# Feature map of a linear-attention branch: min-max on GpSimd, then one fused max-add on VectorE that reads PSUM

## The chip, the cores and the metric

The kernel runs on one core of a Trainium2 chip. A core has a matrix engine (TensorE, PE in the profile), three elementwise engines (VectorE or DVE, ScalarE or ACT, GpSimd or POOL), a queue engine for transfers (SyncE or SP), an on-chip memory of 128 partitions (SBUF) and a matmul result memory of eight banks of 128 x 512 float32 (PSUM). Each engine works through its own instruction list in order; engines wait for each other on semaphores. The metric is the device time of one execution in microseconds (us).

## The reference

Two attention blocks read the same input x (2048 tokens of 512 values, 32 heads of 16) and are mixed by a gate per token. Block A is softmax attention; block B is linear attention with a feature map phi.

```python
def _B_ref(x, wqkv, wo):
    ...
    phi = lambda t: jnp.where(t > 0, t + 1, jnp.exp(t)) + 1e-6
    pq, pk = phi(q), phi(k)
    kv = jnp.einsum("bhsd,bhse->bhde", pk, v)
    z = jnp.einsum("bhsd->bhd", pk)
    num = jnp.einsum("bhqd,bhde->bhqe", pq, kv)
    den = jnp.einsum("bhqd,bhd->bhq", pq, z)[..., None] + 1e-6
    o = num / den
    ...
x = A_x
g = _sigmoid((x * gate_w).sum(-1, keepdims=True))
a = _A_ref(x, A_wqkv, A_wo)
b = _B_ref(x, B_wqkv, B_wo)
return g * a + (1 - g) * b
```

`_A_ref` is plain softmax attention: scores, softmax, weighted sum of v, output projection.

## The kernel before

Most of the work is block A. Its scores are cut into 2048 units of 128 keys x 512 queries of one head. A unit's scores come from one matmul (source Qz, KT; "S" below), which uses 32 rows of the matrix engine, so up to four units run beside each other in one wave. The exponential of a unit is taken on one of two ways:

- on ScalarE: two units at a time out of a pair of PSUM banks, line 750, into a tile P. Banks 0, 1 and 2, 3 are two sets that alternate.
- by bit arithmetic: VectorE adds a constant to one unit and stores it as int16 (line 671, from bank 4 or 5, into a tile Z); read as bfloat16 this is a rough power of two. For each pair of units two shifted copies are then made (line 723 on GpSimd, or line 728 on VectorE), and the weighted sum of the three is the exponential. One pair of units therefore needs two instructions of line 671 and two shifts, wherever these run.

P and Z tiles are then multiplied by v (source P,Vc or Z,Vc; up to four units to a wave, into bank 7). A pair of units on ScalarE gives two such matmuls, a pair on the other way six.

All else is written as *tasks*: Python generators that yield one step at a time, a matmul group on PE or one instruction on another engine, with the tiles it reads and writes. Tasks are the projections of q, k and v, the gate, the 16 maps phi(k) (`t_phik`), the products MT, Z and KV, the 16 maps phi(q) (`t_phiq`), denominators and outputs of block B, and the 16 output blocks (`t_final`, lines 1120 to 1156). A task takes its PSUM bank by ("BANK",) and gives it back by ("FREE", b). While scores are being issued, bank 6 is the one bank that tasks share, so a bank that is held longer holds up the next task; at the end of the score work the other banks are added.

No order is written by hand. A planner in the kernel (the loop from line 1336) keeps a clock for each engine, takes the candidates (S waves, both ways of the exponential, shifts, products with v, task steps), gives each a start by its operands' due times and by the cost that stands in the source as the first argument of `ac`, `dv` and `po`, and appends the one with the earliest start to its engine's list. Which units take which way is decided there, by which engine is free. Gaps on PE are filled with matmuls on a tile `warm` whose result is not used. GpSimd instructions and VectorE's shifts (line 728) are planned so that they don't overlap, and a GpSimd instruction waits for the VectorE instruction ahead of the last shift (`gate`, lines 299 and 1388). A change of one cost or step thus gives a new order on every engine from there on.

The feature map is the generator `phi` (lines 1019 to 1028), which `t_phik` and `t_phiq` run for a 128 x 512 block in bank b: ScalarE writes exp(t) to `eb` (line 1023), VectorE writes max(t, 0) + 1e-6 to `mb` (line 1024) and the bank is free, GpSimd clamps `eb` to at most 1 (line 1026), and GpSimd adds the two into `phiK` (line 1027). There are two buffers of `eb` and of `mb`, so two maps may be under way; `mb` also holds the gate's transposes (line 969).

Of the kernel before, what the change touches and what calls it, by code (L numbers as in the profile page):

```python
# [8 lines left out]
ALU = mybir.AluOpType  # L9
# [117 lines left out]
def bass_gated_mix__mha_block__linear_attn_block__prompt_kernel(  # L127
# [46 lines left out]
    with ExitStack() as es:  # L174
        _cnt = [0]

        def SB(shape, dt, name):
            _cnt[0] += 1
            return es.enter_context(nc.sbuf_tensor(f"{name}_{_cnt[0]}", list(shape), dt))
# [37 lines left out]
        eb = SB([128, 2, 512], FP32, "eb")  # L217
        mb = SB([128, 2, 512], FP32, "mb")
# [13 lines left out]
        def bank(b, n=1):  # L232
            return ps[:, 512 * b:512 * (b + n)]
# [8 lines left out]
        r_bank = [R(f"bank{b}") for b in range(8)]  # L242
# [18 lines left out]
        r_eb = [R(f"eb{i}") for i in range(2)]  # L261
        r_mb = [R(f"mb{i}") for i in range(2)]
# [589 lines left out]
        def dv(dur, fn, reads, writes):  # L852
            return ("OP", DV, dur, fn, reads, writes, None)

        def ac(dur, fn, reads, writes):
            return ("OP", AC, dur, fn, reads, writes, None)

        def po(dur, fn, reads, writes):
            return ("OP", PO, dur, fn, reads, writes, None)
# [159 lines left out]
        def phi(b, dst_ap, dst_res):  # L1019
            yield ("WAIT", lambda: phi_free[0] or phi_free[1])  # L1020
            i = 0 if phi_free[0] else 1
            phi_free[i] = False
            yield ac(480, lambda: nc.scalar.activation(eb[:, i, :], bank(b), ACT.Exp), [r_bank[b]], [r_eb[i]])  # L1023
            yield dv(607, lambda: nc.vector.tensor_scalar(mb[:, i, :], bank(b), 0.0, 1e-6, op0=ALU.max, op1=ALU.add), [r_bank[b], r_eb[i]], [r_mb[i]])  # L1024
            yield ("FREE", b)
            yield po(640, lambda: nc.gpsimd.tensor_scalar(eb[:, i, :], eb[:, i, :], 1.0, 0.0, op0=ALU.min, op1=ALU.max), [r_eb[i]], [r_eb[i]])  # L1026
            yield po(1300, lambda: nc.gpsimd.tensor_tensor(dst_ap, eb[:, i, :], mb[:, i, :], ALU.add), [r_eb[i], r_mb[i]], dst_res)  # L1027
            phi_free[i] = True

        def t_phik(tb):  # L1030
            b = yield ("BANK",)
            for h in range(2):
                yield pe_step(2, 512, [mmt(bank(b), xT[:, cc, 128 * tb:128 * (tb + 1)], wB[:, cc, D:2 * D], start=(cc == 0), stop=(cc == NCC - 1))
                                       for cc in (2 * h, 2 * h + 1)], [r_xT[tb // 4][h], r_wB], [r_bank[b]])
            yield from phi(b, phiK[:, tb, :], [r_phiK[tb]])
            yield ("FLAG", lambda: flags.add(("phik", tb)))
# [38 lines left out]
        def t_phiq(qc, i):  # L1075
            yield ("WAIT", lambda: "z" in flags and "kv" in flags)
            b = yield ("BANK",)
            for h in range(2):
                yield pe_step(2, 512, [mmt(bank(b), wB[:, cc, 128 * i:128 * (i + 1)], xT[:, cc, 512 * qc:512 * (qc + 1)], start=(cc == 0), stop=(cc == NCC - 1))
                                       for cc in (2 * h, 2 * h + 1)], [r_xT[qc][h], r_wB], [r_bank[b]])  # L1080
            yield from phi(b, phiQT[:, 4 * qc + i, :], [r_phiK[4 * qc + i]])
            yield ("FLAG", lambda: flags.add(("phiq", qc, i)))
# [253 lines left out]
        while True:  # L1336
# [53 lines left out]
            if isinstance(c.fns, tuple) and c.fns[0] == "DMA":  # L1390
                _, o, i, sem, tot, lat, rd, wr, tr, chk = c.fns[1]
# [72 lines left out]
```

The softmax here doesn't subtract the row's maximum and nothing guards it: scores larger than these inputs give would overflow.

## Time and profile before

| | |
|---|---|
| median of 5 runs | 690.05 us (689.82 to 690.58) |
| the profiled execution | 690.04 us, of which the span from its first to its last instruction is 688.1 us |
| granted clock of TensorE | 1.000 |
| units of scores on ScalarE (line 750) | 707 instructions of two units each |
| units on the other way (line 671) | 634, with 408 shifts on GpSimd and 226 on VectorE |
| the 32 feature maps | 32 instructions each at lines 1023, 1024, 1026 and 1027 |

The page of the profile gives busy time by engine, the busy share in 40 slices of the span, the chain of work that ended last, and groups of equal instructions (line, engine, operation, written tile <- read tiles, shape, count | busy us, mean ns of one | idle time of that engine just ahead of them, and what ended it). Instructions of one engine overlap at their ends, so a mean duration can be longer than the distance from one to the next. Busy time counts an overlap once.

### The profile page before, as it was taken

To read this page: it belongs to the slowest core of one execution; us is meant where nothing else is said; L and a number is where in the kernel's file an instruction comes from. 1 tells how busy PE (TensorE), PEld (TensorE's weight loads), DVE (VectorE), ACT (ScalarE), POOL (GpSimd) and SP (SyncE) were. 2 spreads that over 40 slices of the span, in tenths; PEclk is the share of its full clock that TensorE was granted. 3 is DMA by queue.
4 is the path that set the end of the run, shared out by engine and by line. 5 is a ranking of instruction groups with operands and counts; after the bars stand their busy time and mean duration, and the time that the engine had idled before them with its cause. 6 is when DMAs were issued, how large, how long until landed. Compare 5 with 4: busy or idle time off the path is not lost.

```text
span 688.1 us, 24162 instructions
## 1 busy us (share of the span) xinstructions
PE 671.5 (98%) x9890; PEld 204.8 (30%) x9923; DVE 607.4 (88%) x1084; ACT 669.2 (97%) x746; POOL 536.8 (78%) x600
## 2 busy tenths in 40 slices
PE   8999999999999999999999999999999999999998
PEld 3323232222323232222333323232333322222222
DVE  6899989889988898988889888989889899988995
ACT  5899999999999999999999999999999999999995
POOL 3748888887898879886887888878989985588860
PEclk9999999999999999999999999999999999999999
DMA  6920000000000000000000000000011210000001
GB/s 132 304 62 10 7 5 7 2 10 1 5 8 2 9 4 1 10 2 10 2 11 3 4 9 2 10 2 3 17 25 34 49 25 25 17 10 16 18 17 40
DMA packets 27869, 15.97 MB, mean 23 GB/s; under 512 B 19696, under 2 KB 26736, under 8 KB 27760
## 3 DMA queue, kind: packets, MB, share of 16 engines
q1 hardware_dynamic: 26416, 13.91, 7.5%
q8 instruction: 79, 1.29, 0.8%
q10 hardware_dynamic: 1344, 0.52, 0.3%
q14 instruction: 30, 0.25, 0.1%
HBM read 6.69 MB, written 2.10 MB: 13 GB/s over the span
## 4 chain that ended last, share of the span: by engine, by line
PE 64%; ACT 23%; issue 9%; POOL 1%; DVE 1%; ACTq 0%; POOLq 0%; DVEq 0%
PE ps L355 49%; ACT P L750 22%; PE ps L361 15%; ACT eb L1023 1%; POOL Z L723 1%; DVE Z L671 1%; DVE Zbd L1057 0%; PE ps L878 0%; DVE T L988 0%; ACTq L1407 0%; POOL T L1011 0%; ACT KT L900 0%; ACT wA L1150 0%; POOL warm L408 0%; ACT gt L974 0%
## 5 line engine op out<-in xcount | busy, mean ns | idle before, releaser
L750 ACT ACTIVATE P<-ps 128x1024 bf16<-128x1024 f32 x707 | 656.8, 1129 | 5.1 <-PE ps L355 5.1
L723 POOL TENSOR_TENSOR Z<-Z,mcon 128x512 int32<-128x512 int32 x408 | 423.0, 1061 | 105.0 <-DVE Z L671 66.3
L671 DVE TENSOR_SCALAR Z<-ps 128x512 int16<-128x512 f32 x634 | 424.6, 682 | 57.8 <-PE ps L355 52.5
L355 PE MATMUL ps<-Qz,KT 32*128 32x512 bf16 x2048 | 276.3, 384 | 3.3 <-ACT P L750 2.0
L355 PE MATMUL ps<-Z,Vc 128*17 128x512 bf16 x1902 | 269.8, 382 | 1.4 <-DVE T L988 1.1
L355 PE MATMUL ps<-P,Vc 128*17 128x512 bf16 x1414 | 246.2, 383 | 0.5 <-POOL Z L723 0.3
L355 PEld LDWEIGHTS ps<-Qz,KT 32*128 32x128 bf16 x2048 | 68.8, 91 | 263.8 <-ACT P L750 244.5
L728 DVE TENSOR_SCALAR Z<-Z 128x1024 int16<-128x1024 int16 x226 | 92.5, 438 | 0.6
L355 PEld LDWEIGHTS ps<-Z,Vc 128*17 128x17 bf16 x1902 | 61.4, 88 | 71.4 <-issue 42.2
L355 PE MATMUL ps<-warm 128*32 128x512 bf16 (+18 forms) x670 | 68.1, 333 | 5.8 <-issue 3.8
L355 PEld LDWEIGHTS ps<-P,Vc 128*17 128x17 bf16 x1414 | 55.8, 88 | 58.2 <-issue 45.8
L1027 POOL TENSOR_TENSOR phiK<-eb,mb 128x512 bf16<-128x512 f32 x32 | 41.0, 1282 | 7.3 <-DVE Z L671 3.0
L361 PE MATMUL ps<-xT,wA 128*32 128x512 bf16 x512 | 43.5, 383 | 0.2 <-ACT P L750 0.2
L355 PEld LDWEIGHTS ps<-warm 128*32 128x32 bf16 (+1 forms) x703 | 23.0, 95 | 20.6 <-issue 14.1
L988 DVE STREAM_TRANSPOSE T<-ps 128x512 f32<-128x512 f32 x32 | 22.8, 712 | 4.7 <-PE ps L355 4.0
L955 POOL TENSOR_SCALAR Vc<-Vc 128x576 bf16<-128x576 bf16 x32 | 21.8, 682 | 5.8 <-DVE Vc L952 2.0
L1026 POOL TENSOR_SCALAR eb<-eb 128x512 f32<-128x512 f32 x32 | 20.0, 624 | 8.0 <-ACT P L750 2.7
L1024 DVE TENSOR_SCALAR mb<-ps 128x512 f32<-128x512 f32 x32 | 21.8, 681 | 2.5 <-ACT eb L1023 1.9
L1011 POOL TENSOR_TENSOR T<-T,rg 128x256 bf16<-128x256 f32 x31 | 19.5, 628 | 5.1 <-DVE Z L728 1.6
L361 PE MATMUL ps<-wA,xT 128*32 128x128 bf16 x1024 | 21.8, 220 | 1.6 <-issue 1.4
L361 PE MATMUL ps<-xT,wB 128*32 128x512 bf16 x256 | 22.9, 383 | 0.0
L1023 ACT ACTIVATE eb<-ps 128x512 f32<-128x512 f32 x32 | 22.8, 713 | 0.0
(80 smaller groups left out, 304.9 us busy)
## 6 DMA issues: line engine op xcount, KB each, us to landing
Qz<-QT SPq DMA_DIRECT2D x120, 16.0 KB, 1.8
wA<-in_A_wqkv_dram SPq DMA_DIRECT2D x1, 1536.0 KB, 7.8
wB<-in_B_wqkv_dram SPq DMA_DIRECT2D x1, 1536.0 KB, 12.0
xnat<-in_A_x_dram SPq DMA_DIRECT2D x3, 512.0 KB, 13.0
out_dram<-outt SPq DMA_DIRECT2D x12, 128.0 KB, 1.7
woA<-in_A_wo_dram SPq DMA_DIRECT2D x1, 512.0 KB, 13.2
woB<-in_B_wo_dram SPq DMA_DIRECT2D x1, 512.0 KB, 9.2
out_dram<-wA SPq DMA_DIRECT2D x4, 128.0 KB, 1.8
```

What stands on the lines that cost most here:

```text
L355: return lambda: nc.tensor.matmul(o, lhsT=l, rhs=r, start=start, stop=stop, skip_group_check=sg)
L361: h = nc.tensor.matmul(o[32 * j:32 * j + 32], lhsT=l[:, 32 * j:32 * j + 32], rhs=r, start=start, stop=stop, skip_group_check=True)
L671: return C(DV, 400, 533 * n + 74, lambda: nc.vector.tensor_scalar(o, i, ZB, 0.0, op0=ALU.add, op1=ALU.max), [r_bank[b] for b in bks], r_Z[ ...
L723: return C(PO, 400, 70 + 484 * n, lambda: nc.gpsimd.tensor_tensor(Z[:, z, 0:512 * n].bitcast(I32), Z[:, z0, 0:512 * n].bitcast(I32), mcon[ ...
L728: return C(DV, 450 if hot else 300, 69 + 134 * n, lambda: nc.vector.tensor_scalar(Z[:, z, 0:512 * n], Z[:, z0, 0:512 * n], float(m), None, ...
L750: return C(AC, 500, 427 * n + 49, lambda: nc.scalar.activation(P[:, slot, 0:512 * n], bank(b0, n), ACT.Exp, scale=ESC), [r_bank[b0 + k] fo ...
L955: yield po(690, lambda k=k: nc.gpsimd.tensor_scalar(Vc[:, k, vs].rearrange("p a b c -> p (a b c)"), Vc[:, 0, vs].rearrange("p a b c -> p ( ...
L988: yield dv(607, lambda: nc.vector.transpose(T1[:, a, :], bank(7)), [r_bank[7]], [r_T1[a]])
L1023: yield ac(480, lambda: nc.scalar.activation(eb[:, i, :], bank(b), ACT.Exp), [r_bank[b]], [r_eb[i]])
L1024: yield dv(607, lambda: nc.vector.tensor_scalar(mb[:, i, :], bank(b), 0.0, 1e-6, op0=ALU.max, op1=ALU.add), [r_bank[b], r_eb[i]], [r_mb[i]])
L1026: yield po(640, lambda: nc.gpsimd.tensor_scalar(eb[:, i, :], eb[:, i, :], 1.0, 0.0, op0=ALU.min, op1=ALU.max), [r_eb[i]], [r_eb[i]])
L1027: yield po(1300, lambda: nc.gpsimd.tensor_tensor(dst_ap, eb[:, i, :], mb[:, i, :], ALU.add), [r_eb[i], r_mb[i]], dst_res)
```

## The change

In `phi`, the instruction of line 1024 goes, with its write of `mb`. GpSimd's clamp now follows ScalarE's exponential directly and clamps at 1 + 1e-6. VectorE then runs one instruction on the bank and on the clamped `eb`: (max(t, 1e-6)) + eb, which writes `phiK`. For t > 0 that is t + 1 + 1e-6, for t <= 0 it is 1e-6 + exp(t), as before. The bank is given back behind this instruction. GpSimd's add is gone. `mb` stays allocated, for the gate.

```diff
             yield ac(480, lambda: nc.scalar.activation(eb[:, i, :], bank(b), ACT.Exp), [r_bank[b]], [r_eb[i]])
-            yield dv(607, lambda: nc.vector.tensor_scalar(mb[:, i, :], bank(b), 0.0, 1e-6, op0=ALU.max, op1=ALU.add), [r_bank[b], r_eb[i]], [r_mb[i]])
+            yield po(640, lambda: nc.gpsimd.tensor_scalar(eb[:, i, :], eb[:, i, :], 1.0 + 1e-6, 0.0, op0=ALU.min, op1=ALU.max), [r_eb[i]], [r_eb[i]])
+            yield dv(607, lambda: nc.vector.scalar_tensor_tensor(dst_ap, bank(b), 1e-6, eb[:, i, :], op0=ALU.max, op1=ALU.add),
+                     [r_bank[b], r_eb[i]], dst_res)
             yield ("FREE", b)
-            yield po(640, lambda: nc.gpsimd.tensor_scalar(eb[:, i, :], eb[:, i, :], 1.0, 0.0, op0=ALU.min, op1=ALU.max), [r_eb[i]], [r_eb[i]])
-            yield po(1300, lambda: nc.gpsimd.tensor_tensor(dst_ap, eb[:, i, :], mb[:, i, :], ALU.add), [r_eb[i], r_mb[i]], dst_res)
             phi_free[i] = True
```

In the changed kernel the clamp is line 1024 and the fused instruction line 1025; all other line numbers stay. The planner makes a new order with it.

## The prediction

> **What bounds the kernel now.** I read the busy shares first, then the slices. TensorE, ScalarE and VectorE are all close to full, so the shares alone decide nothing.
>
> ```profile
> span 688.1 us, 24162 instructions
> PE 671.5 (98%) x9890; PEld 204.8 (30%) x9923; DVE 607.4 (88%) x1084; ACT 669.2 (97%) x746; POOL 536.8 (78%) x600
> ACT  5899999999999999999999999999999999999995
> ```
>
> So I next asked for busy time in stretches (columns: TensorE, its weight loads, VectorE, ScalarE, GpSimd, each with its count, then clock, DMA share, GB/s) and for what ScalarE's line 750 waits for.
>
> ```profile
> 10.00:40.00 30.00, 28.13 (x546) 10.59 (x542) 26.01 (x46) 26.28 (x29) 19.02 (x23) 1.00 0.73 228
> 40.00:80.00 40.00, 39.52 (x549) 11.64 (x551) 38.22 (x74) 39.98 (x46) 27.18 (x34) 1.00 0.04 11
> 130.00:180.00 50.00, 49.31 (x695) 14.99 (x691) 45.14 (x79) 50.00 (x58) 42.80 (x46) 1.00 0.02 5
> 330.00:380.00 50.00, 48.55 (x1011) 16.85 (x1012) 43.80 (x77) 48.96 (x54) 43.79 (x48) 1.00 0.02 5
> 530.00:580.00 50.00, 48.78 (x780) 15.00 (x781) 46.01 (x82) 50.00 (x56) 39.71 (x44) 1.00 0.16 33
> 670.00:688.00 18.00, 15.29 (x230) 5.29 (x226) 10.42 (x20) 10.87 (x13) 1.04 (x1) 1.00 0.12 38
> ```
> ```profile
>   PE ps L355: 5.1, 6
> ...
>   PEld ps L355: 246.5, 626
> ```
>
> ScalarE has no idle time at all in the stretches shown from 40 us on, but for 1.04 us around 330 to 380 (where MT, Z and KV are made). In the whole run it waited 5.1 us for scores, 6 times. TensorE's weight loads for scores, in the other direction, waited 626 times for ScalarE to leave a bank. That is the pacer: ScalarE sets the speed, TensorE keeps up with it. The end of the run I read in the timeline (start, length, engine, line; first ScalarE, then TensorE).
>
> ```profile
> 662.91 16.79 ACT L750 ACTIVATE P<-ps 128x1024 bf16<-128x1024 f32 x18
> 683.40 0.59 ACT L1150 CAST wA<-ps 128x512 bf16<-128x512 f32 x1 [3.70 <-PE ps L361]
> ```
> ```profile
> 679.81 0.39 PE L355 MATMUL ps<-P,Vc 128*17 128x512 bf16 x4
> 680.03 0.60 PE L361 MATMUL ps<-woB,xnat 128*32 128x512 bf16 x8
> 680.46 0.82 PE L361 MATMUL ps<-woA,OAT 128*32 128x512 bf16 x12
> ...
> 684.25 1.03 PE L361 MATMUL ps<-woA,OAT 128*32 128x512 bf16 x16
> ```
>
> The last exponential ends at 662.91 + 16.79 = 679.70; the last product with v follows at 679.81, then output projections without a gap to 685.28, one cast and the last store. Time therefore is: 10.19 us until the first exponential (from ScalarE's timeline), 669.5 us in which ScalarE is full but for some 4.6 us, 8.4 us behind it, and 690.04 - 688.1 = 1.94 us outside the span.
>
> **The change part by part.** The rows that price it:
>
> ```profile
> L750 ACT ACTIVATE P<-ps 128x1024 bf16<-128x1024 f32 x707 | 656.8, 1129 | 5.1 <-PE ps L355 5.1
> L723 POOL TENSOR_TENSOR Z<-Z,mcon 128x512 int32<-128x512 int32 x408 | 423.0, 1061 | 105.0 <-DVE Z L671 66.3
> L671 DVE TENSOR_SCALAR Z<-ps 128x512 int16<-128x512 f32 x634 | 424.6, 682 | 57.8 <-PE ps L355 52.5
> L1027 POOL TENSOR_TENSOR phiK<-eb,mb 128x512 bf16<-128x512 f32 x32 | 41.0, 1282 | 7.3 <-DVE Z L671 3.0
> L1024 DVE TENSOR_SCALAR mb<-ps 128x512 f32<-128x512 f32 x32 | 21.8, 681 | 2.5 <-ACT eb L1023 1.9
> ```
> ```profile
> L1111 DVE TENSOR_TENSOR wA<-ps,wA 128x512 bf16<-128x512 f32 x16 | 10.8, 678 | 0.9 <-DMA xnat<-wA 0.7
> L1015 DVE STREAM_TRANSPOSE OAT<-T 128x512 bf16<-128x512 bf16 x15 | 10.6, 703 | 0.0
> ```
>
> *Removed: GpSimd's add, line 1027.* 32 x 1.282 = 41.0 us of GpSimd. By itself worth nothing, since GpSimd is 78% busy and nothing on ScalarE waits for it. Its worth lies in what the planner puts there. I counted the instructions of both built programs. Line 750 goes from 707 to 701, line 671 from 634 to 646; both make 2048 units (2 x 707 + 634 = 2 x 701 + 646). Shifts on GpSimd go from 408 to 435, on VectorE from 226 to 211. So 12 units leave ScalarE. GpSimd gets back 27 x 1.04 = 28 of its 41 us (423.0 / 408 = 1.04 each) and ends near 524 us busy.
>
> *What that takes off the pacer.* The 18 exponentials at the end take 16.79 us, the last of them 1.13 (the row's mean), so one starts every (16.79 - 1.13) / 17 = 0.921 us. Six fewer: 6 x 0.921 = 5.5 us. This lies on the path that sets the end for its whole length, as the stretches show.
>
> *VectorE.* 32 instructions of line 1024 become 32 fused ones. The trace has none of that form. Nearest is line 1111: one float32 operand from PSUM, one from SBUF, bfloat16 out, 678 ns, next to 681 for line 1024. From below, the shortest single line 671 took 620 ns; from above, a pass for each operand would put a second start interval on top. Two instructions of line 671 back to back take 1.29 us, the later one lasting 0.68, so an interval is about 0.60 us and the cost up to 32 x 0.60 = 19 us of VectorE. I take no difference, because line 1111 is nearest by its operands. Beside it VectorE gets 12 more of line 671 (12 x 0.60 = 7.2 us) and 15 fewer shifts (92.5 us / 226 = 0.41 each, 6.1 us): 1 us more on 607. That lies in its 58 us of waiting for score matmuls.
>
> [...]
>
> *GpSimd's clamp* is the same form as before, 32 of about 0.62 us (20.0 us / 32). Moved ahead of VectorE, it no longer waits for VectorE's read.
>
> *The new wait: VectorE for GpSimd.* Behind the waiting fused instruction stand line 671 (which frees banks 4 and 5 for score waves) and the transposes of bank 7; TensorE waits for both, and ScalarE for TensorE. Bounds: at best less than nothing, since the 1.9 us of line 1024's waits for ScalarE go; at worst a clamp stands behind a shift that has just begun each time, 32 x 1.04 = 33 us. The nearest row for a VectorE instruction that waits for GpSimd is line 1015: 15 of them, 0.0 us idle ahead. The planner gives VectorE other work until the clamp is due. I take 0. Cover for a miss is VectorE's 10% idle share and the score set that is queued while the other is exponentiated; without it every wait goes to ScalarE one to one.
>
> *The bank is held longer.* In the first map, ScalarE ended at 76.63 us and VectorE's read at 77.44; GpSimd was in a shift until 77.74 and ended its clamp at 78.43. A fused instruction would have ended near 79.2, so some 1.75 us more, up to 56 us of bank 6 over 32 maps. It sets the end only if tasks pile up behind the last exponential. In the new order the 16th map has 244 instructions of line 750 ahead of it (245 before) and the second sixteen span 129 (131 before), so the maps' spacing is unchanged. The last map has 167 of line 750 behind it instead of 182, still 150 us. At the end three more matmul groups of four stand behind the last product with v, 26 instead of 23. A group takes 0.216 us (684.25 to 685.28 is four of them with the last one's 0.39). Cost: 3 x 0.216 = 0.65 us.
>
> *TensorE as second sum.* Products with v rise from 3316 to 3340 matmuls, six groups or +1.3 us; score waves fall from 706 to 701, -1.1 us; fill falls by 2.8 us by its columns (48.2 to 45.4 at 2.4 columns a nanosecond, the rate that 512 columns in 0.216 us give). TensorE's list is about 2.6 us shorter, so it doesn't become the limit in place of ScalarE.
>
> Sum: 688.1 - 5.5 + 0.65 = 683.2 us of span, plus 1.94 = 685.2 us, against 690.04 in the profiled run and a median of 690.05.
>
> **The rivals.**
>
> 1. *Forecast: ScalarE stays full and has six fewer.* 685.2 us, with its own range from 682.6 (ScalarE's 4.6 us of idle time shrinks by half as well) to 688.4 (3 us of new idle time). For it: full stretches before and after every map. Chance 0.69.
> 2. *The gain is given back.* The new chain ScalarE, GpSimd, VectorE costs ScalarE about 0.15 us a map, 32 x 0.153 = 4.9 us, or bank 6 is late and MT, Z and KV stretch the one place where ScalarE already idles. Time about 690. For it: the gap between the two sets of maps grows from 149 to 161 of line 750. Against: line 1015's zero. Chance 0.08 (within 0.2%, 1.4 us, about what a measurement of this kernel can tell from no change).
> 3. *Slower: VectorE stands behind a late GpSimd.* Place: the 32 fused instructions, between 77 and 515 us. Price: if VectorE stands half of a shift (0.52 us) each time and two thirds reach ScalarE, 32 x 0.35 = 11 us, so 685.2 + 11 = 696. It decides from 0.15 us a map that reaches ScalarE; above 0.20 it is slower than the band. For it: VectorE is 90% busy there, the planner's costs for GpSimd (1038 ns for a shift) are a bit short of the measured 1061, and GpSimd itself waits for VectorE (66.3 us for line 671), so lateness can go round. Against: ScalarE is also slower than planned (903 ns planned, 921 measured), which gives GpSimd the same grace. A fused instruction at twice the interval would come out at the same place, 19 us on VectorE and half of it on ScalarE: 695. Together 0.23.
>
> **How the numbers follow.** The prediction is rival 1's 685.2 us. The range runs from 682.6 to 694.0: it takes in all of 1 and 2 and the lower part of 3, and leaves most of 3's stated 696 out. Faster by over 0.2% is 1 (0.69), the same 2 (0.08), slower 3 (0.23).
>
> **What would show it.** In the changed profile: line 750 x701 with an idle time ahead of it of 5 us or little more; ScalarE busy near 663.7; fused instructions of 0.68 us with under 3 us of idle time ahead in total; last exponential near 674.2; GpSimd near 524 us busy. I am wrong if line 750 idles over 10 us, if the fused instruction takes over 1 us, or if VectorE's idle time ends on line 1024 of GpSimd for several microseconds.

## The result, and the profile after

The changed kernel takes 687.25 us (median of 25 runs, 685.95 to 690.62) against 690.33 us for the kernel before (median of 49 runs): a ratio of 0.9956, 95% interval 0.9946 to 0.9966. It is faster by 0.44%, 3.1 us. The prediction was 685.2 us, a gain of 4.9.

In 16 of the 25 runs the mean of TensorE's granted clock is 1.000 ("full clock" below; median 686.82 us), and in nine it is 0.995 to 0.998 (median 689.22 us), the profiled run among them (688.84 us, span 686.8), so the profile shows some 2 us more than a run at full clock takes.

The page of the changed kernel; line 1024 is now GpSimd's clamp:

```profile
span 686.8 us, 24180 instructions
PE 669.2 (97%) x9920; PEld 203.6 (30%) x9945; DVE 609.1 (89%) x1081; ACT 664.4 (97%) x740; POOL 522.0 (76%) x595
L750 ACT ACTIVATE P<-ps 128x1024 bf16<-128x1024 f32 x701 | 652.1, 1134 | 8.2 <-PE ps L355 8.2
L723 POOL TENSOR_TENSOR Z<-Z,mcon 128x512 int32<-128x512 int32 x435 | 449.0, 1057 | 108.1 <-DVE Z L671 84.5
L671 DVE TENSOR_SCALAR Z<-ps 128x512 int16<-128x512 f32 x646 | 432.7, 683 | 53.4 <-PE ps L355 47.5
L1024 POOL TENSOR_SCALAR eb<-eb 128x512 f32<-128x512 f32 x32 | 20.2, 632 | 25.6 <-ACT eb L1023 7.9
```

Six exponentials fewer took 656.8 - 652.1 = 4.7 us off ScalarE's line 750. But its idle time rose from 5.1 to 8.2 us. The same stretches as before tell where (columns as in the prediction):

```profile
10.00:40.00 30.00, 28.02 (x544) 10.69 (x545) 25.98 (x47) 26.36 (x29) 19.06 (x23) 1.00 0.74 228
130.00:180.00 50.00, 49.38 (x733) 15.03 (x732) 45.45 (x83) 50.00 (x58) 38.55 (x43) 1.00 0.02 5
330.00:380.00 50.00, 48.69 (x1007) 16.86 (x1004) 44.45 (x76) 48.76 (x54) 43.66 (x46) 1.00 0.02 5
530.00:580.00 50.00, 47.06 (x940) 16.59 (x934) 44.55 (x76) 47.17 (x52) 42.19 (x48) 0.97 0.28 49
```

Start, middle and maps are as before. The new idle time is in one place, 530 to 580 us, where ScalarE was 50.00 of 50 us busy before and is now 47.17; there the clock is 0.97 and DMA moves 49 GB/s instead of 33. The last exponential ends at 677.81 us instead of 679.70, and 9.0 us follow it (8.4 before).

What stands between 530 and 580 us is the output of block B: 16 products that VectorE normalises (line 1111, into one of two OBn buffers) and that SyncE's queue then transposes by DMA (line 332). The queue before and after (start, length, engine, line, count):

```profile
492.61 54.73 SPq L332 DMA_TRANSPOSE xnat<-wA  x14
...
556.49 1.27 SPq L332 DMA_TRANSPOSE xnat<-wA  x1
...
566.49 1.27 SPq L332 DMA_TRANSPOSE xnat<-wA  x1
```
```profile
533.84 38.20 SPq L332 DMA_TRANSPOSE xnat<-wA  x16
```

They used to be spread over 74 us and now all fall into 38. How one of them reaches ScalarE can be read off four engines of the changed kernel, VectorE first, then TensorE, then ScalarE:

```profile
563.81 0.69 DVE L1111 TENSOR_TENSOR wA<-ps,wA 128x512 bf16<-128x512 f32 x1 [1.87 <-DMA xnat<-wA]
```
```profile
564.56 0.41 PE L361 MATMUL ps<-KVbd,phiK 128*32 128x128 bf16 x16 [1.36 <-DVE wA L1111]
...
565.22 0.61 PE L355 MATMUL ps<-P,Vc 128*17 128x512 bf16 x3
```
```profile
565.33 1.02 ACT L750 ACTIVATE P<-ps 128x1024 bf16<-128x1024 f32 x1 [1.07 <-PE ps L355]
567.03 1.02 ACT L750 ACTIVATE P<-ps 128x1024 bf16<-128x1024 f32 x1 [0.67 <-PE ps L355]
568.52 3.80 ACT L750 ACTIVATE P<-ps 128x1024 bf16<-128x1024 f32 x4 [0.47 <-PE ps L355]
```

A transpose issued at 558.75 us lands 4.9 us later, where the median is 2.5 and the planner counts on 2.5. VectorE stands 1.87 us for its buffer. Bank 6 is not emptied, so TensorE, in order, stands 1.36 us ahead of the next product; score waves behind it are late. Then something follows that costs as much again: TensorE's matmuls take 0.61 us instead of 0.39 for a while, and ScalarE waits at three exponentials in a row, 1.07 + 0.67 + 0.47 = 2.2 us. The granted clock (last but two columns):

```profile
563.00:565.00 2.00, 0.64 (x22) 0.33 (x18) 1.19 (x2) 1.26 (x2) 2.00 (x3) 1.00 0.28 28
565.00:567.00 2.00, 2.00 (x21) 0.43 (x23) 1.90 (x4) 1.02 (x1) 2.00 (x3) 0.54 0.33 66
567.00:569.00 2.00, 1.78 (x26) 0.74 (x26) 1.38 (x2) 1.50 (x2) 2.00 (x3) 0.61 0.32 66
```

This is one run. None of the changed kernel's runs at full clock was profiled, and in those the second half of the chain, the fall of the clock, has no part.

Nothing stands ahead of the late transpose in SyncE's queue. But the DMA engines carried something else beside the transposes of q1 (queue, packets, MB, share; 556 to 566 us):

```profile
q1 hardware_dynamic: 2392, 0.58, 44.2%
q8 instruction: 1, 0.02, 0.9%
q14 instruction: 2, 0.02, 0.5%
```

The one packet of q8, which the page calls "instruction", has 16 KB and runs from 560.11 to 561.49 us, while the transpose is under way. Block B has 224 transposes in the 14 profiles of this case. In 97 of them such a packet was under way between 1 us behind the issue and the landing, and all 50 that took over 3.5 us to land are among these; the other 127 took 2.43 us (median), 3.49 at most. Three of the 50 are in the kernel before and three in the changed one, so the change didn't make transposes late; it made a late one matter. No run moves these packets: the link is seen, not tested.

### The profile page after: what moved, and what is told of

Its sections match the earlier page's. It is cut to its first block, busy times and chain, and to the rows that moved or that the text cites. A ratio compares the mean times of both kernels' runs of the same rounds, so it can differ in the third digit from the quotient of the medians.

```text
span 686.8 us, 24180 instructions
## 1 busy us (share of the span) xinstructions
PE 669.2 (97%) x9920; PEld 203.6 (30%) x9945; DVE 609.1 (89%) x1081; ACT 664.4 (97%) x740; POOL 522.0 (76%) x595
## 4 chain that ended last, share of the span: by engine, by line
PE 71%; ACT 17%; issue 6%; DVE 4%; DMA 1%; POOL 1%; ACTq 0%; DVEq 0%; POOLq 0%
PE ps L355 54%; PE ps L361 16%; ACT P L750 16%; DVE Z L671 2%; DMA xnat<-wA 1%; DVE Z L728 1%; DVE wA L1111 0%; POOL Z L723 0%; ACT eb L1023 0%; DVE Zbd L1057 0%; DVE T L988 0%; PE ps L878 0%; POOL eb L1024 0%; DVE KT L902 0%; DVE OAT L1015 0%
## 5 line engine op out<-in xcount | busy, mean ns | idle before, releaser
L750 ACT ACTIVATE P<-ps 128x1024 bf16<-128x1024 f32 x701 | 652.1, 1134 | 8.2 <-PE ps L355 8.2
L723 POOL TENSOR_TENSOR Z<-Z,mcon 128x512 int32<-128x512 int32 x435 | 449.0, 1057 | 108.1 <-DVE Z L671 84.5
L671 DVE TENSOR_SCALAR Z<-ps 128x512 int16<-128x512 f32 x646 | 432.7, 683 | 53.4 <-PE ps L355 47.5
L355 PE MATMUL ps<-Z,Vc 128*17 128x512 bf16 x1938 | 275.1, 383 | 1.5 <-DVE T L988 1.5
L355 PE MATMUL ps<-P,Vc 128*17 128x512 bf16 x1402 | 248.9, 384 | 0.3 <-ACT P L750 0.3
L728 DVE TENSOR_SCALAR Z<-Z 128x1024 int16<-128x1024 int16 x211 | 88.3, 441 | 0.7
L355 PE MATMUL ps<-warm 128*32 128x512 bf16 (+15 forms) x676 | 64.9, 333 | 4.6 <-issue 2.6
L1024 POOL TENSOR_SCALAR eb<-eb 128x512 f32<-128x512 f32 x32 | 20.2, 632 | 25.6 <-ACT eb L1023 7.9
L361 PE MATMUL ps<-phiK,xnat 128*32 128x512 bf16 x256 | 22.8, 382 | 0.0
L361 PE MATMUL ps<-wB,xT 128*32 128x512 bf16 x256 | 22.3, 382 | 0.0
```

Of the source, the lines that this page charges most:

```text
L355: return lambda: nc.tensor.matmul(o, lhsT=l, rhs=r, start=start, stop=stop, skip_group_check=sg)
L361: h = nc.tensor.matmul(o[32 * j:32 * j + 32], lhsT=l[:, 32 * j:32 * j + 32], rhs=r, start=start, stop=stop, skip_group_check=True)
L671: return C(DV, 400, 533 * n + 74, lambda: nc.vector.tensor_scalar(o, i, ZB, 0.0, op0=ALU.add, op1=ALU.max), [r_bank[b] for b in bks], r_Z[ ...
L723: return C(PO, 400, 70 + 484 * n, lambda: nc.gpsimd.tensor_tensor(Z[:, z, 0:512 * n].bitcast(I32), Z[:, z0, 0:512 * n].bitcast(I32), mcon[ ...
L728: return C(DV, 450 if hot else 300, 69 + 134 * n, lambda: nc.vector.tensor_scalar(Z[:, z, 0:512 * n], Z[:, z0, 0:512 * n], float(m), None, ...
L750: return C(AC, 500, 427 * n + 49, lambda: nc.scalar.activation(P[:, slot, 0:512 * n], bank(b0, n), ACT.Exp, scale=ESC), [r_bank[b0 + k] fo ...
```

## The experiments

Twelve kernels were run. "At full clock" is the median of the runs whose granted clock was 1.000, with their number, "idle" is the idle time of line 750 between 530 and 580 us in the profiled run, "first" the issue of the first of the 16 transposes; ratios are of all runs, against the kernel before on the same chip. Beside e1 to e4 that kernel takes 690.18 us at full clock, beside e5 to e8 690.05, beside e9 to e12 690.19.

| run | line 750 | median us | at full clock | ratio (95%) | idle | first |
|---|---|---|---|---|---|---|
| before | 707 | 690.33 | | | 0 | 492.6 |
| changed | 701 | 687.25 | 686.82 (16 of 25) | 0.9956 (0.9946 to 0.9966) | 2.8 | 533.8 |
| e1 add kept | 705 | 701.6 | (0 of 5) | 1.0143 (1.0116 to 1.017) | 5.8 | 546.6 |
| e2 three buffers | 701 | 686.27 | 685.05 (4 of 8) | 0.9927 (0.9901 to 0.9952) | 0 | 537.3 |
| e3 bank held | 707 | 694.52 | 691.93 (2 of 12) | 1.0047 (1.0027 to 1.0068) | 0.9 | 524.8 |
| e4 late landing planned | 701 | 686.8 | 686.5 (5 of 9) | 0.9946 (0.9926 to 0.9965) | 0 | 534.7 |
| e5 before, repaired | 706 | 689.97 | 689.89 (9 of 11) | 1.0002 (0.9993 to 1.0011) | 0 | 501.1 |
| e6 changed, repaired | 702 | 691.19 | (0 of 9) | 1.0012 (1.0001 to 1.0023) | 4.4 | 541.0 |
| e7 add kept, repaired | 706 | 693.66 | 691.44 (1 of 6) | 1.0049 (1.0036 to 1.0061) | 3.6 | 537.1 |
| e8 bank held, repaired | 707 | 695.56 | (0 of 6) | 1.0083 (1.0064 to 1.0103) | 4.0 | 529.6 |
| e9 before, queue planned | 708 | 692.0 | 691.48 (7 of 12) | 1.0022 (1.0008 to 1.0035) | 0 | 500.5 |
| e10 changed, queue planned | 702 | 688.41 | 687.31 (2 of 6) | 0.9962 (0.9947 to 0.9976) | 0 | 538.9 |
| e11 add kept, queue planned | 705 | 689.82 | 689.66 (9 of 12) | 0.9989 (0.9977 to 1.0001) | 0.1 | 537.9 |
| e12 bank held, queue planned | 707 | 691.09 | 689.45 (6 of 12) | 0.9998 (0.9983 to 1.0013) | 0 | 531.2 |

**e1 and e3: one part of the change at a time.** e1 gives GpSimd an add back, into an unused buffer; the map stays fused. e3 is the kernel before with the bank given back later.

```diff
 # e1, on the changed kernel, end of phi
-            yield ("FREE", b)
+            yield ("FREE", b); yield po(1300, lambda: nc.gpsimd.tensor_tensor(mb[:, i, :], eb[:, i, :], eb[:, i, :], ALU.add), [r_eb[i]], [r_mb[i]])
 # e3, on the kernel before
-            yield ("FREE", b)
             yield po(640, lambda: nc.gpsimd.tensor_scalar(eb[:, i, :], eb[:, i, :], 1.0, 0.0, op0=ALU.min, op1=ALU.max), [r_eb[i]], [r_eb[i]])
+            yield ("FREE", b)
```

> The changed kernel, with a GpSimd add of 128x512 float32 per map added back (it writes the unused buffer mb, nothing reads it), 32 in all. Its built program has 705 of line 750, 638 of line 671 and 409 shifts on GpSimd, against 701, 646 and 435 of the changed kernel and 707, 634 and 408 of before. Theory (the gain is GpSimd's freed time, spent on shifts, so that units leave ScalarE): the time goes back up by about 4 x 0.93 = 3.7 us over the changed kernel's undisturbed 686.8, so 690 to 691. Rival (the gain comes from the fused map itself or from a lucky new order): it stays at 686 to 688.

> The kernel before with one line moved: the bank of a map is given back behind GpSimd's clamp instead of behind VectorE's read. 707 of line 750 as before. It does the change's bank hold alone. Theory (holding the bank costs ScalarE nothing directly, but makes block B's outputs bunch up later): 690 to 691.5, ScalarE's idle time up to 2 us more than 5.1, transposes packed in less than 74 us. Rival (the bank hold is what ate the rest of the gain): 692 or more.

Both missed, upwards. e1 took 701.6 us, not 690 to 691; e3 took 694.52, by its rival's measure (691.93 at full clock, in two runs). In e1 line 750 idled 14.3 us, 5.8 of it between 530 and 580 and 3.1 at 380 us, where TensorE stood 1.8 us for the last Zbd (line 1057; 160 ns are planned for each of its four instructions). e3 idled 9.5 us, 3.3 of it at that same place. So a single experiment in this kernel carries a new order with it, and the order's own stalls can be larger than what is asked. The two stalls had to be taken out first.

The row of Zbd in the kernel before needs a second look:

```profile
L1057 DVE TENSOR_SCALAR Zbd<-zmask,ps 128x8 bf16<-128x8 f32 x4 | 2.3, 629 | 0.0
```

The mean of 629 ns is one of 0.99, 1.08, 0.22 and 0.22 us. In all 14 profiles, the ten of these instructions with GpSimd idle beside them but for their first 0.06 us took 0.22 us; the other 46 took 0.31 to 1.15 us, and each ended 0.03 us behind the end of a GpSimd shift (line 723). In e1 and e3 all four were of that kind, in the kernel before two. By these times it is the shift beside it that stretches Zbd, though no run tests this by itself, and the 630 ns that e5 to e12 plan for it fit neither case.

**e2 and e4: the wait for the transposes.** e2 gives OBn a third buffer, from the idle half of mb. Exponentials, shifts and GpSimd's list stay as in the changed kernel. e4 also plans 5500 ns for a transpose.

```diff
-        r_OBn = [R(f"OBn{i}") for i in range(2)]
+        r_OBn = [R(f"OBn{i}") for i in range(3)]
...
-            yield ("WAIT", lambda: ("den", qc) in flags and (qb < 2 or ("ob", qb - 2) in flags))
+            yield ("WAIT", lambda: ("den", qc) in flags and (qb < 3 or ("ob", qb - 3) in flags))
...
-            a, o = qc % 2, qb % 2
+            a, o = qc % 2, qb % 3
```

> The changed kernel with a third buffer for block B's normalised output (tile OBn, taken from the idle half of mb), ahead of the DMA transpose. Number and order of the exponentials, shifts and GpSimd instructions are those of the changed kernel; only TensorE's and VectorE's order between about 533 and 571 us differs. Theory (a transpose that lands late holds VectorE, then a bank, then TensorE and ScalarE, and the gap lowers TensorE's granted clock): VectorE's wait for the transposes (2.2 us) goes, line 750's idle time falls from 8.2 to about 5.4 us, the clock is 1.000, the time is 685.0 to 686.5 without a second cluster of runs near 689. Rival (the idle time of ScalarE between 540 and 570 us is the denser block of tasks itself): idle time stays near 8 us, time 687.

> As e2, and the planner is told that a transpose takes 5500 ns instead of 2500 before its buffer is free. Same 701 of line 750; 147 instead of 137 matmul records behind the last score wave. Theory: idle time of line 750 about 5 us as in e2; the tail is up to 2.5 groups or 0.5 us longer; 685 to 686.5. Rival (bunching itself): near 687.

e2, the same stretch and line 1111:

```profile
530.00:580.00 50.00, 49.32 (x1044) 17.72 (x1042) 47.95 (x83) 50.00 (x56) 45.07 (x50) 1.00 0.31 51
```
```profile
L1111 DVE TENSOR_TENSOR wA<-ps,wA 128x512 bf16<-128x512 f32 x11 | 7.5, 682 | 0.4 <-PE ps L361 0.4
```

The block of transposes is just as dense (0.31 DMA share, 51 GB/s), VectorE no longer waits for one (nor ahead of the five of line 1111 that write mb), ScalarE is full. The rival, density itself, falls. e2's line 750 still idled 8.2 us in the profiled run, as in the changed kernel, but elsewhere: 24.44 us busy in the stretch 10 to 40 us instead of 26.36, at a clock of 0.89. That place has nothing to do with the change: in all 14 profiles TensorE has a gap of 1.1 to 1.5 us near 28 us, and in seven (e1, e2, e3, e7 and e10 to e12) the clock falls behind it. So the expectation of a clock of 1.000 was wrong: half of e2's eight runs are below it. At full clock e2 takes 685.05 us and the changed kernel 686.82, so a third buffer gives some 1.8 us, and e2 beats both kernels. (The two did not run side by side; the kernel before differs by 0.14 us between the chips of e1 to e12.) e4 has the same full stretch, and a longer tail: 10.1 us behind the last exponential instead of 9.0. Its 686.8 us miss the expected range by 0.3.

**e5 to e8: the three maps with both stalls repaired, as I thought.** Third buffer (in a part of wB that is idle by then) and 630 ns for Zbd, on the kernel before, the changed one, e1 and e3.

```diff
-                yield dv(160, lambda i=i: nc.vector.tensor_scalar(Zbd[:, i, :], zmask[:], bank(b)[:, i:i + 1], None, op0=ALU.mult),
+                yield dv(630, lambda i=i: nc.vector.tensor_scalar(Zbd[:, i, :], zmask[:], bank(b)[:, i:i + 1], None, op0=ALU.mult),
...
-        wB = SB([128, NCC, 3 * D], BF16, "wB")
+        wB = SB([128, NCC, 3 * D], BF16, "wB"); OBx.append(wB[:, 0, D:2 * D])
```

> The kernel before with two repairs that have nothing to do with the feature map: a third buffer for block B's output ahead of the transpose (in a part of wB that is idle by then), and the planned cost of the four Zbd instructions (line 1057) set to 630 instead of 160 ns (the trace has 629). 706 of line 750. Theory (the two stalls, behind late transposes and behind Zbd, are set by the order and hit any new order; before had little of them): 688 to 690, line 750's idle time 4 to 5 us. Rival (the repairs are worth several us in every order): 686 or less.

> The changed kernel with the same two repairs. 702 of line 750, four fewer than e5. Theory: 4 x 0.93 = 3.7 us less than e5 with equal idle time of ScalarE, so 684.5 to 686.5. Rival (the fused map or the held bank has a cost of its own on ScalarE): within 2 us of e5.

> e1 with the same two repairs: the fused map, and beside it a GpSimd add per map that nothing reads. 706 of line 750, as in e5. Theory (all the gain is GpSimd's freed time): the time of e5 within 1.5 us. Rival (e1's 701.6 us came from the extra instruction's own disturbance, not from stalls of its order): 695 or more, with idle time of line 750 over 10 us. Other rival (the fused map is worth something by itself): near e6.

> e3 with the same two repairs: unfused map, bank given back behind GpSimd's clamp. 707 of line 750. Theory (the held bank costs nothing by itself; e3's 3 us were stalls behind Zbd and the transposes): e5 + 0.9 us, within 1 us. Rival (the hold itself costs): 2.5 us or more over e5.

Only e5 came out as expected. e6 to e8 idle 3.6 to 4.4 us in the block of transposes in spite of three buffers. SyncE's queue and VectorE in e6 say why:

```profile
523.25 17.68 SPq L336 DMA_DIRECT2D Qz<-QT  x16
541.03 2.57 SPq L332 DMA_TRANSPOSE xnat<-wA  x2
```
```profile
535.89 0.69 DVE L1111 TENSOR_TENSOR wA<-ps,wA 128x512 bf16<-128x512 f32 x1 [0.23 <-PE ps L361]
...
543.61 0.69 DVE L1111 TENSOR_TENSOR wA<-ps,wA 128x512 bf16<-128x512 f32 x1 [2.60 <-DMA xnat<-wA]
```

The first block is ready at 535.89 + 0.69 = 536.6 us, its transpose is issued at 541.0: it stood in the queue behind the loads of Qz, which need 0.59 us each there, eight to a round. The planner counts 60 ns for each. e7 and e8 have the same picture with eight loads (in e7 the transpose behind them also landed late, after 4.0 us), as in e8:

```profile
555.64 6.03 SPq L336 DMA_DIRECT2D Qz<-QT  x8
561.71 1.27 SPq L332 DMA_TRANSPOSE xnat<-wB  x1
```
```profile
564.33 0.69 DVE L1111 TENSOR_TENSOR wB<-ps,wA 128x512 bf16<-128x512 f32 x1 [3.03 <-DMA xnat<-wB]
```

In e1 too the first transpose, at 546.62, stands behind eight loads, from 541.58 to 546.5 us, and VectorE waits 3.5 us for it: the larger of e1's two stalls. A third buffer, which e6 to e8 have, didn't take such waits away.

**e9 to e12: the queue planned as measured.** To e5 to e8, 600 ns for a load of Qz, 1200 ns for a transpose, 5000 ns until it has landed.

```diff
-                fin = dma(SP, o, i, sem, tot, lat, reads=rd, writes=c.writes, transpose=tr, name=c.name)
+                fin = dma(SP, o, i, sem, tot, lat, reads=rd, writes=c.writes, transpose=tr, name=c.name, issue=1200.0 if tr else 600.0)
```

> e5, and the planner also gets what SyncE's queue needed in the traces: 600 ns for each of the eight loads of a Qz (60 were planned, the traces have 590), 1200 ns to issue a transpose (60 planned, 1190 measured) and 5000 ns until it has landed (2500 planned). 708 of line 750. Theory (the idle time of ScalarE between 530 and 580 us comes from transposes that stand in SyncE's queue behind Qz loads, or land late, in whatever order the planner makes): idle time of line 750 about 5 us, 690 to 691.5. Rival (the order itself does it, however the queue is planned): idle time 8 us or more.

> e6 with the queue's times planned as in e9. 702 of line 750, six fewer than e9. Theory: idle time of line 750 about 5 us instead of 9.3, no idle time of more than 0.5 us between 530 and 580 us, 685 to 687, so 5 us below e9. Rival (the fused map has a cost of its own on ScalarE that the order shows): 688.5 or more.

> e7 with the queue's times planned as in e9: fused map and a GpSimd add per map that nothing reads. 705 of line 750. Theory (the gain is GpSimd's freed time): 3 x 0.93 = 2.8 us over e10, so 688 to 690, idle time of line 750 about 5 to 6 us. Rival (the fused map is worth 2 us or more beside that): within 1 us of e10. Other rival (the added instruction disturbs by itself): 692 or more.

> e8 with the queue's times planned as in e9: unfused map, bank held until GpSimd's clamp is done. 707 of line 750. Theory (the held bank costs ScalarE only through the later, denser block of transposes): with that queue planned it falls from 695.6 to 689.5 to 691.5, within 1.5 us of e9. Rival (a held bank costs by itself): 693 or more.

Line 750 of e9, e10, e11 and e12:

```profile
L750 ACT ACTIVATE P<-ps 128x1024 bf16<-128x1024 f32 x708 | 657.4, 1136 | 5.0 <-PE ps L355 4.9
```
```profile
L750 ACT ACTIVATE P<-ps 128x1024 bf16<-128x1024 f32 x702 | 652.7, 1137 | 5.6 <-PE ps L355 5.6
```
```profile
L750 ACT ACTIVATE P<-ps 128x1024 bf16<-128x1024 f32 x705 | 655.8, 1128 | 6.7 <-PE ps L355 6.4
```
```profile
L750 ACT ACTIVATE P<-ps 128x1024 bf16<-128x1024 f32 x707 | 657.5, 1146 | 5.6 <-PE ps L355 5.6
```

Idle time is 5 to 7 us in all four, and none of note between 530 and 580. e12 fell from 695.56 to 691.09 us and lies within 1 us of e9, on the better side: once the queue is planned, no cost of the held bank shows. e9 itself missed its 690 to 691.5 by 0.5 us and is 2.0 us slower than e5 (on another chip), with two exponentials more. Between e9 and e10, equal but for the change, lie 692.0 - 688.41 = 3.6 us (4.2 at full clock) at six exponentials less; 5.5 would be their worth. e10 missed its 685 to 687: four of its six runs have a clock under 1.000 (the other two took 687.12 and 687.5), and its tail is 10.6 us (9.4 in e9, 9.0 in the changed kernel; about half of the latter difference is four more matmul groups behind the last product with v). e11 lies between: 1.4 us over e10 at three exponentials more, 2.2 us under e9; at full clock, 2.4 over and 1.8 under. So keeping an add takes back about half of the gain here, as it does half of the six exponentials. That share changes with the order: by the built orders it is four of six without repairs (707, 705, 701) and all four in e5 to e7 (706, 706, 702). Why the planner finds room in the fused map even with an add kept was not tested.

## Why the prediction was right in sign and too large

- *ScalarE is the pacer, six exponentials fewer: 5.5 us.* Right in kind: 701 of line 750, ScalarE busy 664.4 us (about 663.7 was named), 4.7 us off line 750. But the last exponential ended at 677.81 us, where 674.2 was named: 3.1 us of new idle time ate most of the gain in that run.
- *GpSimd's freed add is what buys this.* Half right. GpSimd ended at 522.0 us busy (524 forecast), with 27 more shifts. But with an add kept, part of the gain stays: e11 gives back 1.4 of e10's 3.6 us over e9 (2.4 of 4.2 at full clock).
- *The fused instruction costs what line 1024 did.* Right:

```profile
L1025 DVE SCALAR_TENSOR_TENSOR phiK<-ps,eb x32: 623/682/692, 77.6 to 522.3; 128x512 bf16<-128x512 f32 x32
```

  (least, median and greatest ns.) The upper bound of 19 us, my estimate of a second start interval of 0.60 us on each of the 32, had no part: the longest took 692 ns.
- *The new wait of VectorE for GpSimd: 0.* Right: no idle time at all ahead of line 1025, in the changed kernel and in every fused variant here. Rival 3 with its 696 us falls; the waits went to GpSimd, which idles 25.6 us ahead of its clamp (8.0 before) and is 76% busy.
- *TensorE's list 2.6 us shorter.* 2.3 us of busy time.
- *The tail: 0.65 us for three more groups.* Measured 0.6 (9.0 against 8.4).
- *The bank is held longer, and "sets the end only if tasks pile up behind the last exponential".* This is the step that failed. I looked at the maps' spacing and at the end of the run, and not at what is queued for the same bank behind the maps, nor at SyncE's queue, which the output steps use. In all three orders with the bank held and the unfused map (e3, e8, e12), block B's first transpose comes 28 to 32 us later than in the kernel it was made from (before, e5, e9), and in the changed kernel 41 us later; the last stays near 570. So the 16 outputs fall into half the time, one late transpose is no longer absorbed, and TensorE and its clock pass it on. Cost in the changed kernel: 3.1 us more idle time in the profiled run, 1.8 us by e2 in runs at full clock. The term that the sum lacked is thus ScalarE's new idle time, put at nothing there. With that wait gone e2 measures 685.05 us at full clock, 5.1 less than the 690.18 of the kernel before on the same chip, close to the forecast gain of 4.9; e4, with the wait gone as well but the longer tail, gains 3.7.
- *Rival 2* named this region's tasks and a late bank 6, but priced them to the end of the gain; they ate about a third.
- *The range.* 682.6 to 694.0 us would have held no change at all, so that the time fell inside says little; the terms above are the test. The ends of rival 1 are also 0.2 to 0.3 us wider than their terms give: 685.2 - 4.6 / 2 = 682.9 and 685.2 + 3 = 688.2.

Left open: whether the 16 KB packets are what makes transposes late; how the 1.8 us come about at full clock; and where the clock dips in the other eight of the nine runs below it, of which there is no profile (the gap near 28 us is a candidate).

## What to carry to other kernels

When an edit holds a shared buffer longer, follow every later user of that buffer to its own queue, DMA issues included, and ask what a denser stretch does there. In a kernel whose order comes from a planner, one experiment tells little until the costs that the planner gets wrong are known: print the idle time of the pacer by stretch for each run, and compare variants only once their stalls are gone. A stall's price is not its length: in the changed kernel's profile a gap of 1.4 us on TensorE cost ScalarE 2.2. And read the least and the greatest time of a group before planning with its mean: Zbd's 629 ns was no instruction's time.

## What the runs showed of the hardware

- *The clock fell behind some gaps of TensorE, not behind each.* In the changed kernel, with matmuls idle for 1.36 us, from 563.2 to 564.56, the granted clock was 0.54 from 565 to 567 us, 0.61 from 567 to 569 and 1.00 from 569 on; in e6 it was 0.50 between 545 and 550 after a gap of TensorE of 2.3 us. Of the 14 gaps of 1.1 to 1.5 us near 28 us seven were followed by a fall, seven (one in the kernel before, of 1.40 us) were not. The six gaps of 1.8 to 3.3 us in the 14 profiles all were.
- *An issue held SyncE's queue.* A load of Qz (16 KB) held it 0.59 us (median, in the kernel before as in the changed one), a DMA transpose 1.23 in the changed kernel (median; 1.19 to 2.10).
- *A small VectorE instruction lasted until the GpSimd instruction beside it had ended.* Zbd, on 128 x 8 elements with a scalar per partition from PSUM, took 0.22 us alone and up to 1.15 us beside shifts, ending 0.03 us behind one. Line 671 (128 x 512 from PSUM), with shifts beside it as well, took 0.69 us at most in the kernel before.
